# A fused attention and feed-forward kernel on one core: weight conversion listed as seven single operations, the first two parts of w_in by column halves, and the list in another order

## The chip, the cores and the metric

The kernel runs on one core of a Trainium2 chip. The time is the device time of one execution in microseconds (us), as the median of several runs. The core has a matrix engine (TensorE, PE in the profile, with PEld for its weight loads), a vector engine (VectorE, DVE), a scalar engine (ScalarE, ACT), a general one (GpSimd, POOL) and an engine that issues transfers (SyncE, SP). Each works through its own queue in order and waits on semaphores for the others. Operands stand in on-chip memory (SBUF), matmul results in banks of PSUM; transfers from and to DRAM are DMAs.

## The reference

```python
# attention: q, k, v, alpha of shape (4, 8, 768, 48), float32
for t in range(S):
    state = alpha[:, :, t, :, None] * state + np.einsum('bhd,bhe->bhde', k[:, :, t], v[:, :, t])
    y[:, :, t] = np.einsum('bhd,bhde->bhe', q[:, :, t], state)
# bridge: (B,H,S,D) -> (B*S, H*D), 3072 tokens of 384
x = attn_out.transpose(0, 2, 1, 3).reshape(B * S, H * D)
# feed-forward: w_in (384, 2048) and w_out (2048, 384), float64
h = np.maximum(x @ w_in, 0.0)
return (h * h @ w_out).astype(np.float32)
```

The state decays by alpha in each row and step, so a chunk of 128 steps is computed at once with cumulative sums of log(alpha).

## The kernel before, in words

**Blocks and groups.** The attention is cut into 24 blocks n: chunk n // 4 of 128 time steps of batch n % 4. Four blocks are a group g of 512 tokens, the unit of the feed-forward part; there are six groups. All 24 blocks of a head's state go in sequence for their batch, so block n needs the state that block n - 4 left.

**The list.** The program is one list of words, `ORDER`, such as `load:5:q` or `ha:0`. A word names a step, a Python function that issues a few instructions, and its numbers. The list is run once from front to back, with the scheduler in manual mode, so the list is the order of each engine's queue; there is no planner and no cost in the kernel. What the list can't say are the waits: they follow from the data, from the rotation of buffers, and from one more rule. The loads of blocks 4 to 7 and all loads of w_in parts are `behind_newest`: they wait until the TensorE instruction that was listed last before them has run.

**Steps of a block.** `load:n:a`, `:q`, `:k`, `:v` are the loads on SyncE. `ln` (ScalarE) takes the log of alpha, `cs` (TensorE) sums it along time, `eb` and `ei` (ScalarE, L540) give exp of plus and minus the sum, `mq` and `mk` (VectorE, L548) scale q and k by them, `dl`, `de`, `bl`, `br` carry the last row. `qT`, `kT` and `turned_one` transpose on TensorE, `qc`, `kc` and `half_copied` (ScalarE) copy the result out of PSUM. `sc` and `kv` (TensorE) are scores and state sums, `one_masked` (VectorE) masks scores, `us`, `sa`, `sb` (VectorE, L705) update the state. `y_states`, `y_inner`, `yb` (TensorE) give y for a pair of blocks, and twelve `moved:n:p:i` (ScalarE, L779) copy that y, transposed, into x, the input of the feed-forward part, for the pair n and n + 1.

**Weights.** w_in and w_out come as eight parts each (0 to 7 are w_in, 8 to 15 w_out). `load_weights:i` brings a part of 768 KB into one of four raw buffers. As the engines have no float64, the conversion works on the two 32-bit words of each number, for all 768 numbers of a partition at once: `first` is two VectorE operations on the high word (the exponent, L422, and the mantissa bits, L426), `middle` two ScalarE operations (the exponent moved up, L435, and the low word scaled, L438), `second` three VectorE operations (the sign, L444, the two mantissa words joined, L448, the product, L451).

**Feed-forward.** Group 0 has its first layer in plain fp32 matmuls: `ha:j` for the first 256 tokens (blocks 0 and 1), `hb:j` for the others, `hf:j` for all 512; `ra`, `rb`, `rf` and `qa`, `qb`, `qf` are relu and square on ScalarE. j is one of 16 slices of the hidden layer; j // 2 is the part of w_in that it needs. Some later j of group 0, and all of the other groups, are split into faster fp32r matmuls: `cast_w`, `rest_w`, `diff_w` make three pieces of a weight part (`wb`, `wl`, `wd`), `split_x`, `rest_x`, `diff_x` three of x, and `in_x` and `in_y` multiply them. `in_scaled`, `in_added`, `in_post`, `in_square` finish h, `split_h`, `rest_h`, `diff_h` split it (`ha`, `hl`, `hd` in the profile), and `out_x`, `out_y` are the second layer, with `out_plain` as its fp32 form. `kept_l`, `kept_d` and `fetch` move pieces of the weights to DRAM and back. `warm` is a dummy matmul of the start. All matmuls are recorded at line L350, a wrapper, so they are told apart by the names of their tiles.

In this kernel the first 13 `warm` steps stand ahead of the first `ha`, and conversion of part 0 stands after `y_inner:0`. The buffers: 4 raw, 26 for weight parts (`wt`), 22 for pieces of h (`two`), 2 for `upper`, 8 banks of PSUM.

Of the kernel before, what the change touches and what calls it, by code (L numbers as in the profile page):

```python
# [36 lines left out]
half_copied:q:5:0 half_copied:q:5:1 sc:5 kv:5 load:8:a load:7:k load:7:q split_x:0:0 rest_x:0:0 split_x:0:1  # L37
first:5 rest_x:0:1 cast_w:i:4 split_x:0:2 rest_x:0:2 one_masked:5:0 half_copied:q:6:0 half_copied:k:6:0
load:6:v hb:2 ei:7 diff_x:0:0 rf:6 first:6 one_masked:5:1 us:5 rb:5 qb:5 qa:4 diff_x:0:1 diff_x:0:2 qa:1 hf:7
y_states:4 mk:7 y_inner:4 rb:2 ln:8 sa:5 half_copied:k:6:1 half_copied:q:6:1 sc:6 load:9:a log_high:8 eb:7  # L40
mq:7 turned_one:7 log_rest:8 kv:6 bl:7 rf:7 middle:6 half_copied:k:7:0 second:6 half_copied:q:7:0 hb:4
load:8:k ln:9 log_high:9 half_copied:k:7:1 one_masked:6:1 load:8:q log_rest:9 cs:8 eb:8 ei:8 load:9:k
rest_w:i:4 load:9:q load:7:v hb:1 cs:9 bl:8 mk:8 rb:4 rb:1 half_copied:q:7:1 mq:8 one_masked:6:0 kept_l:i:4
ei:9 load:10:a us:6 eb:9 mk:9 cast_w:i:6 bl:9 hb:3 rb:3 load:11:a turned_one:8 sc:7 mq:9 rest_w:i:6
half_copied:q:8:0 half_copied:q:8:1 half_copied:k:8:0 half_copied:k:8:1 load_weights:7 yb:4 kv:7 turned_one:9
middle:5 diff_w:i:4 kept_d:i:4 in_x:8 half_copied:q:9:0 sa:6 load:10:q kept_l:i:6 diff_w:i:6 kept_d:i:6
half_copied:k:9:0 ln:10 in_x:12 ln:11 second:5 in_x:13 log_high:10 log_rest:10 load_weights:8 one_masked:7:1
one_masked:7:0 in_scaled:8 in_y:8 us:7 log_high:11 half_copied:q:9:1 in_scaled:12 in_scaled:13 cast_w:i:5
first:7 br:4 log_rest:11 sa:7 in_y:12 in_y:13 in_x:9 rest_w:i:5 in_post:12 half_copied:k:9:1 middle:7 cs:11
load:8:v eb:11 in_post:8 second:7 cs:10 ei:10 eb:10 in_scaled:9 kept_l:i:5 diff_w:i:5 kept_d:i:5 in_x:10  # L50
in_scaled:10 in_x:11 in_y:9 cast_w:i:7 rest_w:i:7 qb:0 moved:4:0:0 moved:4:0:1 kept_l:i:7 in_y:10 in_post:10
diff_w:i:7 kept_d:i:7 in_x:14 in_square:12 in_x:15 first:8 in_scaled:11 in_y:11 sb:4 load_weights:9
in_scaled:14 in_y:14 middle:8 moved:4:0:2 in_added:13 in_added:9 moved:4:1:0 moved:4:1:1 in_added:11 second:8
ei:11 moved:4:1:2 in_scaled:15 y_states:6 y_inner:6 moved:4:2:0 moved:4:2:1 sc:8 moved:4:2:2 moved:4:3:0 br:5
load:10:k yb:6 kv:8 qb:1 qb:2 moved:4:3:1 one_masked:8:0 bl:11 moved:4:3:2 one_masked:8:1 us:8 qb:3 first:9
middle:9 moved:6:0:0 in_y:15 in_added:15 moved:6:0:1 moved:6:0:2 second:9 load_weights:10 first:10 moved:6:1:0
# [210 lines left out]
def kernel(  # L267
# [144 lines left out]
    def convert_first(i):  # L412
        if moe_w_in.dtype == FP32:
            return
# [686 lines left out]
```

## Time and profile before

| | us |
|---|---|
| median of 3 runs | 519.35 |
| lowest and highest run | 519.31, 520.91 |
| profiled execution, whole time | 521.08 |
| profiled execution, span from first to last instruction | 519.30 |
| TensorE busy, of the span | 508.6 (98%) |
| VectorE busy | 362.6 (70%) |
| ScalarE busy | 314.4 (61%) |
| chain that ended last: TensorE's share of the span | 88% |
| chain that ended last: VectorE, ScalarE, DMA | 4%, 3%, 2% |
| TensorE clock granted, mean over the span | 0.997 |

The busy time of an engine says how full it was on average, and not which one was late at a given place. For that, the stretches of the span (busy time of each engine in each), the groups of equal instructions with their mean duration, and the instructions of an engine in order of time with what they waited for are read together. In a row of the groups stand the line, the engine, the operation, output and inputs with their shapes and the count; then the busy time in all and the mean of one in ns; then the idle time of the engine just before them and what ended it. In a row of the timeline stand the start and the duration in us, and in brackets the idle time before and what ended it.

### The profile page before, as it was taken

What the parts mean: (1) busy time and instruction counts of PE and PEld (TensorE: products, weight loads), DVE (VectorE), ACT (ScalarE), POOL (GpSimd) and SP (SyncE); (2) the same over time, 40 slices, a digit from 0 to 9 for tenths busy, and PEclk for the clock granted to TensorE, in tenths of its full rate; (3) what the DMA queues carried; (4) which work ended last, traced back from release to release, by engine and by line L of the source; (5) the groups of instructions that cost most, each with busy time, mean ns of one, the idle gap of its engine ahead of it and who ended that gap; (6) DMA issues with size and microseconds to landing.
All of it is one profiled execution on the core that took longest, in us unless ns stands there. A gap on an engine that the chain in (4) does not pass through costs nothing.

```text
span 519.3 us, 13138 instructions
## 1 busy us (share of the span) xinstructions
PE 508.6 (98%) x5404; PEld 432.0 (83%) x5404; DVE 362.6 (70%) x629; ACT 314.4 (61%) x681; POOL 5.4 (1%) x29
## 2 busy tenths in 40 slices
PE   8989999999999999999999999999999999999997
PEld 6676788567778879987899988899987899988997
DVE  3678999998988898635998147597344598126961
ACT  4789999977486673058766247765253775324620
POOL 4000000000000000000000000000000000000000
PEclk9989999999999999999999999999999999999999
DMA  9969898977756668698876479756883744579301
GB/s 161 218 174 249 176 266 269 275 236 217 220 170 196 193 219 255 215 308 199 239 185 184 146 230 287 216 153 174 221 259 124 231 136 143 182 273 404 123 0 61
DMA packets 140762, 106.27 MB, mean 205 GB/s; under 512 B 109968, under 2 KB 113056, under 8 KB 140704
## 3 DMA queue, kind: packets, MB, share of 16 engines
q1 hardware_dynamic: 140704, 105.45, 70.1%
q8 instruction: 42, 0.69, 0.6%
q14 instruction: 16, 0.13, 0.1%
HBM read 88.10 MB, written 17.33 MB: 203 GB/s over the span
## 4 chain that ended last, share of the span: by engine, by line
PE 88%; DVE 4%; ACT 3%; DMA 2%; issue 1%; POOL 0%; DVEq 0%; ACTq 0%; POOLq 0%
PE o L350 40%; PE h L350 36%; PE sckv L350 4%; PE y L350 4%; PE cs L350 2%; PE T L350 2%; DMA a_in<-in_alpha_dram 1%; PE warm L350 1%; DMA q_in<-in_q_dram 1%; ACT x L779 1%; DVE hid L802 1%; DVE power L444 1%; DVE w_out L451 0%; DVE w_in L451 0%; DVE w_out L448 0%
## 5 line engine op out<-in xcount | busy, mean ns | idle before, releaser
L350 PE MATMUL h<-xa,wb 128*128 128x512 f32 x264 | 76.4, 397 | 0.8 <-ACT ks L754 0.6
L350 PE MATMUL h<-xl,wl 128*128 128x512 f32 x264 | 74.5, 390 | 0.0
L350 PE MATMUL h<-xd,wd 128*128 128x512 f32 x264 | 69.6, 397 | 0.0
L779 ACT COPY x<-y 32x256 f32<-32x256 f32 (+3 forms) x144 | 50.9, 366 | 16.9 <-PE y L350 14.6
L350 PEld LDWEIGHTS h<-xa,wb 128*128 128x128 f32 x264 | 48.8, 188 | 12.3 <-ACT ks L754 1.0
L350 PEld LDWEIGHTS h<-xl,wl 128*128 128x128 f32 x264 | 49.6, 188 | 11.0 <-DVE xl L848 0.2
L350 PEld LDWEIGHTS h<-xd,wd 128*128 128x128 f32 x264 | 48.7, 188 | 11.0 <-ACT h L900 0.5
L802 DVE TENSOR_TENSOR hid<-h,hid 128x512 f32<-128x512 f32 x44 | 29.7, 687 | 40.2 <-PE h L350 40.1
L350 PE MATMUL o<-wb,ha 128*128 128x384 f32 x168 | 56.9, 339 | 0.1
L350 PE MATMUL o<-wd,hd 128*128 128x384 f32 x320 | 56.9, 334 | 0.0
L350 PE MATMUL o<-wl,hl 128*128 128x384 f32 x168 | 56.2, 335 | 0.0
L350 PEld LDWEIGHTS o<-wd,hd 128*128 128x128 f32 x320 | 55.7, 188 | 0.3
L350 PE MATMUL o<-wb,hx 128*128 128x384 f32 x152 | 51.2, 337 | 0.0
L350 PE MATMUL o<-wl,hx 128*128 128x384 f32 x152 | 50.8, 334 | 0.0
L898 ACT ACTIVATE hid<-h 128x512 f32<-128x512 f32 x44 | 26.3, 598 | 38.8 <-PE h L350 38.7
L923 ACT ACTIVATE hid<-h 128x512 f32<-128x512 f32 x44 | 25.8, 598 | 36.4 <-PE h L350 36.1
L802 DVE TENSOR_TENSOR osb<-o,osb 128x384 f32<-128x384 f32 x24 | 12.9, 555 | 44.7 <-PE o L350 30.9
L350 PE MATMUL o<-w_out,hid 128*128 128x384 f32 x128 | 44.0, 491 | 0.0
L845 ACT ACTIVATE ha<-hid 128x512 fp32r<-128x512 f32 x42 | 26.1, 632 | 22.4 <-DVE hid L918 12.0
L900 ACT ACTIVATE h<-h 128x512 f32<-128x512 f32 x44 | 25.6, 591 | 22.8 <-PE h L350 22.6
L350 PEld LDWEIGHTS o<-w_out,hid 128*128 128x128 f32 x128 | 23.7, 189 | 15.9 <-DVE w_out L451 1.0
L848 DVE SCALAR_TENSOR_TENSOR hl<-ha,hid 128x512 fp32r<-128x512 f32 x42 | 28.3, 686 | 12.1 <-ACT ha L845 11.9
(113 smaller groups left out, 893.2 us busy)
## 6 DMA issues: line engine op xcount, KB each, us to landing
wd<-do SPq DMA_DIRECT2D x38, 384.0 KB
wd<-di SPq DMA_DIRECT2D x36, 384.0 KB
wl<-li SPq DMA_DIRECT2D x36, 384.0 KB
wl<-lo SPq DMA_DIRECT2D x34, 384.0 KB
raw<-in_moe_w_in_dram SPq DMA_DIRECT2D x8, 768.0 KB
raw<-in_moe_w_out_dram SPq DMA_DIRECT2D x8, 768.0 KB
v_in<-in_v_dram SPq DMA_DIRECT2D x24, 192.0 KB
out_dram<-osb SPq DMA_DIRECT2D x24, 192.0 KB
```

The costliest lines, as they stand in the source:

```text
L350: newest[:] = [f(*args, **kwargs)]
L444: nc.vector.scalar_tensor_tensor(out=power, in0=hi, scalar=0x80000000, in1=power, op0=ALU.bitwise_and, op1=ALU.bitwise_or,)
L779: copy(out=xT[g][kk].rearrange("a (t c) -> a t c", c=C)[to : to + m, t : t + 2], in_=blk[n]["y"][e][r : r + m, :, p // 2],)
L802: nc.vector.tensor_tensor(out=o, in0=x, in1=z, op=op)
L845: nc.scalar.activation(out=a, in_=x, func=AF.Copy, scale=NEAR * E)
L848: nc.vector.scalar_tensor_tensor(out=l, in0=a.bitcast(FP32), scalar=-1.0 / E, in1=x, op0=ALU.mult, op1=ALU.add)
L898: nc.scalar.activation(out=hid[j], in_=x, func=AF.Copy, scale=E)
L900: nc.scalar.activation(out=x, in_=x, func=AF.Copy, scale=1.0 + E)
L923: nc.scalar.activation(out=h, in_=acc.pop(("h", j)), func=AF.Relu)
```

## The change

`load_weights` becomes `part_loaded:i:h`, and the three conversion steps become seven, one for each instruction: `exponent`, `mantissa` (VectorE), `moved_up`, `lower` (ScalarE), `signed`, `joined`, `valued` (VectorE). Each takes h: 0 and 1 are the left and the right half of the part's columns, 2 is the whole part. In the new list parts 0 and 1 are loaded and converted as halves (two DMAs and fourteen instructions for each, on 384 elements per partition), parts 2 to 15 as wholes. What each instruction computes is the same.

Copies, relus and squares now go through helpers (`copied_to`, `positive_to`, `squared_to`) which give them to the other engine if a word ends with `~`. No word of the new list does, so each stays on the engine it was on; the entries of `AT` that could do the same for a few copies, and left them all on ScalarE, are gone.

The list is written anew: 2428 words for 2348. The words that are not about conversion or weight loads are the same as before, each as many times; their order is another from the first word to the last. All 16 `warm` steps now stand ahead of the first `ha` (13 before). Old and new beginning, up to the copies of the second pair, and the functions:

```diff
 ORDER = """
-load:0:a warm:0 warm:0 warm:0 load:1:a warm:0 ln:0 load:0:q ln:1 warm:0 cs:0 eb:0 load:0:k mq:0 load:1:k cs:1
-ei:0 dl:0 load:0:v qT:0 de:0 warm:0 load:3:a load:1:q mk:0 kT:0 qc:0 kc:0 sc:0 kv:0 load:1:v load:2:a
-one_masked:0:1 load_weights:0 load:2:q load:4:a ei:1 mk:1 one_masked:0:0 eb:1 mq:1 ln:3 us:0 cs:3 ei:3 sa:0
-sb:0 dl:1 kT:1 load:2:k load:5:a kc:1 qT:1 qc:1 sc:1 load:3:q load:3:k kv:1 one_masked:1:0 warm:0 ln:2 cs:2
-ei:2 warm:0 eb:2 one_masked:1:1 load:2:v warm:0 warm:0 eb:3 us:1 y_states:0 y_inner:0 warm:0 mq:2 qT:2 ln:4
-first:0 middle:0 dl:3 load:4:q mk:2 de:1 second:0 cs:4 eb:4 load_weights:1 yb:0 load:4:k load:3:v ei:4 qc:2
-dl:2 kT:2 mk:3 mq:3 ln:5 warm:0 cs:5 de:2 kc:2 sc:2 kv:2 one_masked:2:1 moved:0:0:0 warm:0 moved:0:0:1
-moved:0:0:2 mq:4 load_weights:2 moved:0:1:0 kT:3 moved:0:1:1 moved:0:1:2 moved:0:2:0 moved:0:2:1 de:3
-moved:0:2:2 moved:0:3:0 qT:3 moved:0:3:1 moved:0:3:2 one_masked:2:0 us:2 sa:2 sb:2 load:7:a ha:1 ha:0 bl:4
-warm:0 first:1 mk:4 turned_one:4 kc:3 qc:3 middle:1 load:6:a second:1 ra:0 load_weights:3 ra:1 sc:3 qa:0
-half_copied:q:4:0 half_copied:q:4:1 eb:5 bl:5 kv:3 one_masked:3:0 load:5:k half_copied:k:4:0 half_copied:k:4:1
-warm:0 first:2 warm:0 middle:2 ln:6 ha:3 one_masked:3:1 ha:2 ra:2 ei:5 us:3 cs:6 load:5:q load:4:v y_states:2
-y_inner:2 sc:4 ln:7 load_weights:4 second:2 qa:2 eb:6 load:6:k sa:3 load:6:q ei:6 sa:1 first:3 ra:3 ha:4
-load_weights:5 sb:1 qa:3 mk:5 middle:3 ra:4 sb:3 yb:2 moved:2:0:0 mq:5 moved:2:0:1 moved:2:0:2 moved:2:1:0
-moved:2:1:1 cs:7 moved:2:1:2 moved:2:2:0 moved:2:2:1 moved:2:2:2 turned_one:5 kv:4 second:3 ha:5
-one_masked:4:0 one_masked:4:1 moved:2:3:0 moved:2:3:1 moved:2:3:2 first:4 us:4 half_copied:k:5:0 middle:4 mk:6
-hb:0 bl:6 load:5:v second:4 load_weights:6 hf:6 rb:0 ra:5 qa:5 hb:5 sa:4 mq:6 turned_one:6 half_copied:k:5:1
...
+warm:0 warm:0 load:0:v load:0:a ln:0 cs:0 ei:0 eb:0 load:0:q load:1:a warm:0 load:0:k warm:0 ln:1 load:3:a
+mk:0 dl:0 de:0 load:1:k mq:0 ln:3 load:1:q load:2:a warm:0 load:1:v load:4:a kT:0 warm:0 kc:0 qT:0 qc:0 cs:1
+load:2:k ei:1 eb:1 load:2:q part_loaded:0:0 part_loaded:0:1 cs:3 eb:3 sc:0 kv:0 mq:1 qT:1 dl:1 load:5:a
+load:3:k ln:2 cs:2 one_masked:0:1 one_masked:0:0 us:0 ei:2 sa:0 sb:0 warm:0 mk:1 kT:1 qc:1 kc:1 warm:0 mk:2
+load:3:q load:2:v warm:0 part_loaded:1:0 sc:1 kv:1 one_masked:1:0 one_masked:1:1 us:1 part_loaded:1:1 ei:3
+eb:2 mq:2 ln:4 cs:4 mantissa:0:0 dl:2 load:6:a lower:0:0 joined:0:0 exponent:0:0 eb:4 de:1 ln:5 dl:3 de:3 qT:2
+mk:3 warm:0 warm:0 exponent:0:1 moved_up:0:1 signed:0:1 kT:2 load:3:v kc:2 mantissa:0:1 load:4:q mq:3
+part_loaded:2:2 qc:2 ei:4 bl:4 mantissa:1:0 y_states:0 de:2 y_inner:0 yb:0 moved:0:0:0 exponent:1:0 lower:0:1
+joined:0:1 warm:0 kT:3 moved:0:0:1 moved:0:0:2 kc:3 moved:0:1:0 valued:0:1 moved_up:1:0 load:4:k warm:0 cs:5
+part_loaded:3:2 signed:1:0 moved_up:0:0 signed:0:0 moved:0:1:1 valued:0:0 qT:3 qc:3 exponent:1:1 moved:0:1:2
+sc:2 kv:2 one_masked:2:0 lower:1:0 mantissa:1:1 one_masked:2:1 load:7:a load:5:k warm:0 joined:1:0
+moved_up:1:1 signed:1:1 lower:1:1 joined:1:1 moved:0:2:0 load:5:q valued:1:0 warm:0 warm:0 load:6:k
+moved:0:2:1 moved:0:2:2 moved:0:3:0 moved:0:3:1 moved:0:3:2 ln:6 us:2 sc:3 kv:3 one_masked:3:0 one_masked:3:1
+ha:0 sa:2 us:3 sa:3 valued:1:1 exponent:2:2 load:4:v sb:2 mantissa:2:2 lower:2:2 ei:5 eb:5 ha:1 ha:2 ha:3
+part_loaded:4:2 part_loaded:5:2 cs:6 mk:4 moved_up:2:2 ra:1 qa:1 joined:2:2 ra:2 mq:4 turned_one:4 y_states:2
+mantissa:3:2 lower:3:2 y_inner:2 yb:2 half_copied:k:4:0 eb:6 half_copied:q:4:0 ln:7 cs:7 exponent:3:2
+signed:2:2 valued:2:2 ra:0 ha:5 half_copied:k:4:1 mk:5 moved:2:0:0 sa:1 half_copied:q:4:1 load:6:q
+part_loaded:6:2 mq:5 sb:1 moved_up:3:2 signed:3:2 bl:5 moved:2:0:1 sb:3 moved:2:0:2 moved:2:1:0 joined:3:2
+ei:6 moved:2:1:1 sc:4 kv:4 ha:4 bl:6 ra:3 moved:2:1:2 moved:2:2:0 ra:5 load:5:v load:8:a moved:2:2:1
+one_masked:4:1 moved:2:2:2 moved:2:3:0 moved:2:3:1 qa:5 moved:2:3:2 one_masked:4:0 valued:3:2 us:4
+turned_one:5 exponent:4:2 half_copied:k:5:0 load:7:q sa:4 ra:4 hb:5 mantissa:4:2 half_copied:q:5:0 mk:6
+lower:4:2 joined:4:2 load:7:k moved_up:4:2 signed:4:2 qa:0 split_x:0:0 rest_x:0:0 valued:4:2 load:6:v
+mantissa:5:2 split_x:0:1 hb:1 lower:5:2 qa:3 hb:0 rb:0 mq:6 br:4 qa:2 hf:6 rb:1 load:9:a hb:2 rest_x:0:1
...
 """
...
-    def load_weights(i):
+    def part_loaded(i, h):
         dt = moe_w_in.dtype
         shape = (KM, DF // NW) if i < NW else (NJ // NW, DM)
         if dt == FP32:
             raw = target(i)
         else:
-            raw = raw_pool.tile([128, *shape], dt, tag="raw", name="raw")
-        raws[i] = raw
+            if i not in raws:
+                raws[i] = raw_pool.tile([128, *shape], dt, tag="raw", name="raw")
+            raw = raws[i]
         if i < NW:
-            src = moe_w_in[:, i * DF // NW : (i + 1) * DF // NW]
-            behind_newest(nc.sync.dma_start(out=raw, in_=src.rearrange("(k r) f -> r k f", r=128)))
+            cols = columns(i, h)
+            src = moe_w_in[:, i * DF // NW + cols.start : i * DF // NW + cols.stop]
+            behind_newest(nc.sync.dma_start(out=raw[:, :, cols], in_=src.rearrange("(k r) f -> r k f", r=128)))
         else:
             i -= NW
             src = moe_w_out[i * DF // NW : (i + 1) * DF // NW, :]
             nc.sync.dma_start(out=raw, in_=src.rearrange("(j r) m -> r j m", r=128))
...
+    over = [False]
+    def copied_to(out, x, scale=1.0, vector=False):
+        if vector == over[0]:
+            if scale == 1.0:
+                nc.scalar.copy(out=out, in_=x)
+            else:
+                nc.scalar.activation(out=out, in_=x, func=AF.Copy, scale=scale)
+        elif scale == 1.0:
+            nc.vector.tensor_copy(out=out, in_=x)
+        else:
+            nc.vector.tensor_scalar(out=out, in0=x, scalar1=scale, scalar2=None, op0=ALU.mult)
...
+    def columns(i, h):
+        n = DF // NW if i < NW else DM
+        return slice(0, n) if h == 2 else slice(h * n // 2, (h + 1) * n // 2)
+    def wide(x, i, h):
+        shape = (KM, DF // NW) if i < NW else (NJ // NW, DM)
+        if x in "lo hi":
+            t = raws[i].bitcast(U32).rearrange("a k (f h) -> a k f h", h=2)[:, :, :, x == "hi"]
+        elif x == "w":
+            t = target(i)
+        else:
+            if (x, i) not in half:
+                half[x, i] = (
+                    wt("power", U32, shape) if x == "power"
+                    else cv_pool.tile([128, *shape], U32, tag="upper", name="upper")
+                )
+            t = half[x, i]
+        return t if h == 2 and x in ("w", "power", "upper") else t[:, :, columns(i, h)]
+    def exponent(i, h):
         nc.vector.tensor_scalar(
+            out=wide("power", i, h), in0=wide("hi", i, h), scalar1=20, scalar2=0x7FF,
             op0=ALU.logical_shift_right, op1=ALU.bitwise_and,
         )
+    def mantissa(i, h):
         nc.vector.tensor_scalar(
+            out=wide("upper", i, h), in0=wide("hi", i, h), scalar1=0xFFFFF, scalar2=None, op0=ALU.bitwise_and
+        )
+    def moved_up(i, h):
+        power = wide("power", i, h)
+        nc.scalar.activation(out=power, in_=power, func=AF.Relu, scale=2.0**23, bias=rebias)
+    def lower(i, h):
+        w, lo = wide("w", i, h), wide("lo", i, h)
+        if over[0]:
+            nc.vector.tensor_scalar(out=w, in0=lo, scalar1=2.0**-52, scalar2=1.0, op0=ALU.mult, op1=ALU.add)
+        else:
+            nc.scalar.activation(out=w, in_=lo, func=AF.Copy, scale=2.0**-52, bias=1.0)
+    def signed(i, h):
+        power = wide("power", i, h)
         nc.vector.scalar_tensor_tensor(
+            out=power, in0=wide("hi", i, h), scalar=0x80000000, in1=power,
             op0=ALU.bitwise_and, op1=ALU.bitwise_or,
         )
+    def joined(i, h):
+        w = wide("w", i, h)
         nc.vector.scalar_tensor_tensor(
+            out=w, in0=wide("upper", i, h), scalar=2.0**-20, in1=w, op0=ALU.mult, op1=ALU.add
+        )
+    def valued(i, h):
+        w = wide("w", i, h)
+        nc.vector.tensor_tensor(out=w, in0=w, in1=wide("power", i, h).bitcast(FP32), op=ALU.mult)
...
-    steps["first"], steps["middle"], steps["second"] = convert_first, convert_middle, convert_second
...
-        f, *given = word.split(":")
+        f, *given = word.rstrip("~").split(":")
+        over[0] = word.endswith("~")
```

More of the change, by code (lines that the diff above doesn't have):

```diff
@@ L45 @@
[L45 to L54, printed above, removed]
@@ new lines @@
+one_masked:8:1 moved:4:2:0 moved:4:2:1 in_scaled:15 moved:4:2:2 moved:4:3:0 qb:1 cast_w:i:2 fetch:l:i:5
+in_y:14 in_y:15 out_plain:0:0:6 one_masked:8:0 us:8 fetch:d:i:7 mq:10 load:11:k in_post:14 out_plain:0:2:6
+part_loaded:11:2 exponent:9:2 moved_up:9:2 mantissa:9:2 lower:9:2 bl:11 in_added:15 out_plain:0:3:6
+moved:4:3:1 signed:9:2 out_plain:0:1:6 joined:9:2 valued:9:2 qb:4 moved:6:0:0 load:11:v moved:6:0:1
+moved:6:0:2 part_loaded:12:2 qb:5 fetch:d:i:6 moved:6:1:0 moved:6:1:1 qb:3 out_plain:1:0:6 moved:6:1:2
@@ new lines @@
+fetch:l:i:6 moved:6:2:0 moved:6:2:1 mk:10 out_plain:1:3:6 load:13:a exponent:10:2 load:12:a moved:6:2:2
+out_plain:1:1:6 sa:8 rest_w:i:1 kept_l:i:1 moved_up:10:2 moved:4:3:2 moved:6:3:0 br:7 br:8 mantissa:10:2
+lower:10:2 out_plain:1:2:6 moved:6:3:1 moved:6:3:2 qf:7 mk:11 mq:11 signed:10:2 turned_one:11
+half_copied:q:11:0 half_copied:q:11:1 joined:10:2 valued:10:2 mantissa:11:2 lower:11:2 exponent:11:2
+turned_one:10 half_copied:k:10:0 out_plain:2:1:6 in_post:9 rest_w:i:2 kept_l:i:2 half_copied:k:10:1
@@ L753, in half_copied @@
             blk[n][f"{x}s"] = work(f"{x}s", 2 if x == "k" else 4)
-        nc.scalar.copy(out=blk[n][f"{x}s"][:, :, HALF[h]], in_=blk[n]["T"][h][:, "kq".index(x)])
-    SHARED = {(n, int(p)) for n, ps in enumerate(AT["shared"].split(",")) for p in ps}
+        copied_to(blk[n][f"{x}s"][:, :, HALF[h]], blk[n]["T"][h][:, "kq".index(x)])
     def cells(p):
```

507 lines of the change are left out of this document (244 added, 263 removed).

## The prediction

> **What bounds the kernel now.** I read first the engines' busy time, then the same by stretches of the span, because an average over stages with different limits hides where time is lost, and last the chain that ended last. The first line below is the page's; the others are the stretches (span, then each engine's busy time with its count, clock, DMA share, GB/s) and their sum.
>
> ```profile
> PE 508.6 (98%) x5404; PEld 432.0 (83%) x5404; DVE 362.6 (70%) x629; ACT 314.4 (61%) x681; POOL 5.4 (1%) x29
> ...
> 0.00:10.00 10.00, 7.91 (x56) 5.86 (x60) 2.92 (x5) 5.04 (x11) 5.36 (x29) 1.00 1.04 157
> 10.00:20.00 10.00, 9.29 (x235) 7.05 (x226) 5.88 (x15) 5.72 (x13) 0.00 (x0) 1.00 1.11 215
> 20.00:30.00 10.00, 8.01 (x152) 5.72 (x152) 7.14 (x14) 8.70 (x26) 0.00 (x0) 0.95 0.91 200
> 30.00:40.00 10.00, 10.00 (x122) 7.99 (x124) 7.35 (x12) 7.42 (x17) 0.00 (x0) 0.88 0.64 185
> 40.00:50.00 10.00, 9.22 (x198) 7.17 (x193) 7.93 (x17) 9.29 (x24) 0.00 (x0) 1.00 1.00 223
> 50.00:60.00 10.00, 9.60 (x126) 5.94 (x128) 9.96 (x20) 9.94 (x27) 0.00 (x0) 1.00 0.92 219
> 60.00:70.00 10.00, 10.00 (x304) 8.93 (x296) 9.96 (x19) 8.74 (x23) 0.00 (x0) 1.00 0.85 178
> 70.00:80.00 10.00, 9.96 (x57) 8.03 (x58) 9.97 (x17) 9.63 (x21) 0.00 (x0) 1.00 1.03 317
> 90.00:100.00 10.00, 10.00 (x67) 5.60 (x59) 8.84 (x18) 9.72 (x22) 0.00 (x0) 1.00 1.10 258
> 100.00:120.00 20.00, 20.00 (x157) 13.16 (x156) 18.71 (x29) 16.51 (x36) 0.00 (x0) 1.00 0.74 229
> 160.00:200.00 40.00, 39.42 (x421) 33.12 (x421) 37.51 (x65) 25.06 (x54) 0.00 (x0) 1.00 0.73 224
> 500.00:519.30 19.30, 15.90 (x92) 15.58 (x90) 4.15 (x8) 2.27 (x5) 0.00 (x0) 1.00 0.11 41
> sum 519.30, PE 508.57 PEld 431.96 DVE 362.55 ACT 314.40 POOL 5.36; mean PE 22.11 PEld 18.78 DVE 15.76 ACT 13.67 POOL 0.23
> ```
>
> TensorE (PE) is busy 508.57 of 519.30 us. Its first 60 us hold 54.03 (7.91 + 9.29 + 8.01 + 10.00 + 9.22 + 9.60), so 5.97 idle; the last stretch lacks 3.40, which is the last copy and the store; the 440 us between hold 438.64, so 1.36 idle. The change neither adds nor removes a matmul, so only three things can move: the start, stalls hidden inside "busy" groups, and 1.36 us. What follows TensorE in the start is seen in the other columns: from 50 us on VectorE (DVE) is busy 8.84 to 9.97 of each 10 us and ScalarE (ACT) 8.74 to 9.94, while before that VectorE idles 18.78 of 50 us. VectorE stays near full up to 200 us (18.71 of 20, 37.51 of 40). So the helpers' late start is never made up before the second group of tokens: a microsecond saved on VectorE or ScalarE before 50 us is worth up to a microsecond at the end, and one lost costs the same.
>
> How much TensorE could win at most comes from long unbroken stretches of the chain:
>
> ```profile
> 458.01 21.80 PE h L350 x96
> ...
> 490.22 25.70 PE o L350 x148
> ```
>
> A split matmul of 512 columns costs 21.80 / 96 = 0.227 us, one of 384 costs 25.70 / 148 = 0.174 us. With these, and stretches found in the same way for the small ones, the whole list sums to some 495 us, 6.9 of them the 16 `warm` steps (an estimate). Against 516 us at the last matmul about 20 us are lost, some 16 of them before 90 us. Where, is seen in the instructions in order of time:
>
> ```profile
> 21.74 0.96 DVE L451 TENSOR_TENSOR w_in<-w_in,power 128x768 f32<-128x768 f32 x1
> 28.75 0.56 DVE L422 TENSOR_SCALAR power<-raw 128x768 uint32<-128x768 uint32 x1 [0.66 <-DMA raw<-in_moe_w_in_dram]
> 29.04 4.40 PE L350 MATMUL h<-x,w_in 128*128 128x256 f32 x12
> 36.49 2.75 PE L350 MATMUL h<-x,w_in 128*128 128x256 f32 x12
> 39.92 0.37 SPq L376 DMA_DIRECT2D q_in<-in_q_dram  x1
> 44.19 4.37 ACT L779 COPY x<-y 32x256 f32<-32x256 f32 x12
> 44.97 0.56 DVE L548 TENSOR_TENSOR q_in<-q_in,b 128x384 f32<-128x384 f32 x1 [2.01 <-DMA q_in<-in_q_dram]
> 45.58 0.46 PE L350 MATMUL T<-ident,q_in 64*128 64x64 f32 x8 [0.78 <-DVE q_in L548]
> 47.30 0.96 DVE L451 TENSOR_TENSOR w_in<-w_in,power 128x768 f32<-128x768 f32 x1
> ```
>
> The same 12 instructions of the first layer take 4.40 us at 29.04 and 2.75 at 36.49; the stretch between shows a clock of 0.95 and 0.88, so 1.65 us went to a slow clock and late inputs. The first `ha` waits for the twelve copies `moved:0`, not for weights (the last operation on part 0 ends at 21.74 + 0.96 = 22.70). The load of q for block 5 is issued only at 39.92, because it is ordered behind a matmul listed late; it keeps VectorE waiting 2.01 us at 44.97 and TensorE 0.78 at 45.58. The second half of the tokens, `hb`, waits for the copies `moved:2`, which end at 44.19 + 4.37 = 48.56. Part 3 of w_in is converted at 47.30 + 0.96 = 48.26.
>
> **The change, part by part: halves.** Two parts get twice the instructions. The grouped rows (mean ns) and two neighbouring pairs:
>
> ```profile
> L444 DVE SCALAR_TENSOR_TENSOR power<-raw,power 128x768 uint32<-128x768 uint32 x16 | 15.3, 956 | 4.7 <-ACT power L435 4.5
> L422 DVE TENSOR_SCALAR power<-raw 128x768 uint32<-128x768 uint32 x16 | 8.9, 555 | 0.7 <-DMA raw<-in_moe_w_in_dram 0.7
> L435 ACT ACTIVATE power<-power,rebias 128x768 uint32<-128x768 uint32 x16 | 15.1, 945 | 3.7 <-DVE power L422 3.7
> L548 DVE TENSOR_TENSOR k_in<-k_in,inv 128x384 f32<-128x384 f32 x23 | 12.7, 553 | 0.4 <-DMA k_in<-in_k_dram 0.3
> L540 ACT ACTIVATE b<-cs 128x384 f32<-128x384 f32 x24 | 11.8, 495 | 5.9 <-PE cs L350 5.8
> L705 DVE TENSOR_TENSOR s<-s,last 128x192 f32<-128x192 f32 x20 | 7.1, 353 | 0.2
> ...
> 66.45 0.55 DVE L548 TENSOR_TENSOR k_in<-k_in,inv 128x384 f32<-128x384 f32 x1
> 66.92 0.55 DVE L548 TENSOR_TENSOR q_in<-q_in,b 128x384 f32<-128x384 f32 x1
> ...
> 71.79 0.95 DVE L444 SCALAR_TENSOR_TENSOR power<-raw,power 128x768 uint32<-128x768 uint32 x1
> 72.66 0.96 DVE L448 SCALAR_TENSOR_TENSOR w_in<-upper,w_in 128x768 f32<-128x768 uint32 x1
> ```
>
> Queued back to back, a two-input operation on 384 elements takes 66.92 - 66.45 = 0.47 us and on 768 takes 72.66 - 71.79 = 0.87. Two halves cost 0.94, 0.07 more; three such operations on two parts: 0.4 us. No row shows the one-input form (555 ns) on 384 elements: two halves cost between the whole's price (nothing more) and twice it (0.47 back to back, so 0.47 more). I take a half at 0.30, near the 353 ns of the 192-element row, which makes 0.13 more, times two operations and two parts: 0.5 us. VectorE therefore gets 0.9 us more (0.4 to 2.3). On ScalarE two of 495 stand against one of 945 ns: 4 x 0.05 = 0.2 us. The two extra DMA issues lie on SyncE, which is ahead of the data there.
>
> [...]
>
> **The start in the new order.** Counted in the order of the lists (a block load is 128 x 384 fp32, 196.6 KB, a part 384 x 256 float64, 786.4 KB), part 0 is not early: its last byte is number 3,342 KB in the new load order against 2,752; part 1, 4,914 against 5,111; part 2, 6,290 in both; part 3, 7,273 against 7,469. The three first stretches carry 157, 215 and 200 GB/s, so part 0 lands at about 20 us and part 1, by its row, near 28 (28.75 now). What moves is the gating: q of block 5 stands behind TensorE work of 21.7 us instead of 30.0, so the 2.01 and 0.78 us waits should go. Three waits come in: ScalarE's `ln:5` now stands ahead of `qc:2`, `ei:4` and the first `moved_up` and waits for its load to about 21 us; `mk:3` on VectorE waits for k to about 22, and `mantissa:1:0` for half a part to about 26, with `joined:0:1`, `valued` and the state updates queued behind. Walking the new list with the quoted durations, `moved:0` ends at 32.8 instead of 29.2, so `ha:0` begins some 3 us later than now. But then `ha:0` to `ha:3` run in one piece, with both parts converted and all `warm` steps spent; `yb:2` ends near 40.7 and the 12 `moved:2` copies at 46.8 instead of 48.56, with the same ScalarE work before them (38.0 against 38.1 us of summed durations). That is 1.8 us. VectorE has part 3 converted at 46 to 47.6, 0.7 to 2.3 us earlier, though more work lies ahead (32.8 against 30.3): its idle time falls by about 3 us. I take 1.8, ScalarE's figure, since `hb` needs both.
>
> **From 50 to 200 us.** The new order puts more VectorE work ahead of the same TensorE progress: 104.8 against 102.9 us of summed durations ahead of the first split matmul of token group 1, 157.5 against 154.6 near 151 us of TensorE work. Durations overlap (all sum to 397 us, and the engine is busy 362.55), so these are 1.7 and 2.6 us. The halves' 0.9 is in them. Set against 3 us less idle time, VectorE ends 0.4 to 1.3 us ahead. ScalarE needs 1.5 to 2 us more before the group 1 matmuls near 64 us, against 1.8 won. So of the early gain something between 0 and 1.8 us lives to 200 us; I take 1.0. Splitting each conversion in seven lets other work stand between its operations in both engines; in the old list `second` is three operations in a row (L444, L448 and L451, about 0.96 us each by the rows above) that a k or q scaling must wait out, and TensorE waits for such (0.78 above). The stretches from 60 us hold 1.36 us of named idle time and about 3 us hidden in groups; I take 1.0 off for that, bounds 1.5 us more and 3 off. After 200 us VectorE has slack and both lists do the same work at the same TensorE progress within 4 us, so nothing is taken.
>
> Sum: 1.0 + 1.0 = 2.0 us off. The profiled execution took 521.08 us, its span 519.30 with 1.78 around it; it lies 1.73 above the median of 519.35. So 519.1 for a profiled run like it, and 517.3 for the median.
>
> **Rivals.** *VectorE becomes the bound up to 190 us.* If the three new waits cost what the freed loads save, its idle time stays at 18.8 of the first 50 us, and the 2.6 us of work put ahead is paid in full by `out_x` and `out_y` of group 0: 519.35 + 2.6 = 522.0, up to 526 if `mantissa:1:0` waits 3 us longer than worked out or the one-input halves take 2.3 us. It decides from the point where VectorE's idle time before 50 us exceeds 18. For it: VectorE is at 37.51 of 40 between 160 and 200 us. Against: the 2.01 us wait has a cause that the list removes. 0.35.
>
> *The early gain is absorbed:* TensorE enters group 1 at the time it does now because ScalarE, 9.72 busy between 90 and 100 us, is the limit, and its work did not shrink: 519.3, within 1.5. [...] 0.17.
>
> *The order closes nearly all gaps before 200 us:* both slow groups and the hidden stalls, 7 us: 512.4. For it: 20 us are lost in all. Against: both helpers are full. 0.10.
>
> **Numbers.** About 0.3%, 1.6 us, is what a measurement can tell from no change. The forecast holds 0.38, its own range 515.5 to 518.5; a little of it and most of the absorbed case lie within 0.3%. That gives faster 0.46, same 0.17, slower 0.37. The range from 512 to 526 leaves out half of the large gain and the tail of the slow rival.
>
> **What would show it.** Right: `ha:0` near 32 to 33 us with `ha:1` to `ha:3` behind it without a gap; no DMA wait of 2 us on q; `moved:2` done before 47.5; VectorE idle under 17 us in the first 50; TensorE's busy sum near 507. Wrong: `moved:2` later than 48.6, VectorE idle above 18 us by 50, or TensorE waiting for `hl`, `hx` or `wl` between 100 and 200 us by more than 2 us in all, which is the first rival.

## The result, and the profile after

The changed kernel takes 523.20 us (median of 6 runs, 521.42 to 524.11); the kernel before took 519.33 in the same runs (6 runs). The ratio is 1.0067, with a 95% interval of 1.0044 to 1.0091: slower by some 3.5 us by that ratio (3.9 between the medians), where 517.3 was forecast. The profiled execution of the changed kernel took 524.11 us, the slowest of its six, and its span was 522.30.

The page's busy times and its shares of the chain that ended last, and the same stretches as before (span, then busy time and count of TensorE, its weight loads, VectorE, ScalarE and GpSimd, clock, DMA share, GB/s):

```profile
PE 511.1 (98%) x5404; PEld 432.0 (83%) x5404; DVE 362.0 (69%) x639; ACT 317.1 (61%) x685; POOL 5.3 (1%) x29
...
PE 80%; ACT 9%; DVE 6%; DMA 3%; issue 1%; SPq 0%; DVEq 0%
```

```profile
0.00:10.00 10.00, 6.73 (x28) 4.33 (x29) 2.86 (x5) 3.54 (x8) 5.33 (x29) 1.00 1.05 156
10.00:20.00 10.00, 9.81 (x112) 6.84 (x110) 3.27 (x8) 4.86 (x11) 0.00 (x0) 1.00 1.20 215
20.00:30.00 10.00, 9.87 (x273) 7.99 (x274) 6.65 (x16) 8.04 (x23) 0.00 (x0) 1.00 0.84 193
30.00:40.00 10.00, 8.25 (x121) 6.72 (x114) 9.59 (x24) 9.74 (x23) 0.00 (x0) 1.00 1.07 258
40.00:50.00 10.00, 9.35 (x212) 6.96 (x210) 9.25 (x19) 8.64 (x23) 0.00 (x0) 1.00 0.78 218
50.00:60.00 10.00, 9.91 (x111) 7.10 (x111) 8.07 (x14) 9.93 (x25) 0.00 (x0) 1.00 0.78 171
100.00:200.00 100.00, 98.98 (x993) 74.96 (x991) 91.70 (x149) 70.07 (x141) 0.00 (x0) 1.00 0.67 204
```

TensorE is idle 6.08 us in the first 60 (5.97 before), and its busy time is 2.5 us more for the same matmuls: the loss sits inside "busy" groups. VectorE is busy 31.62 of the first 50 us, so 18.38 idle (18.78 before); the prediction had drawn its line at 17 for right and 18 for wrong. ScalarE is the one that falls behind: 34.81 busy by 50 us against 36.17, and 9% of the chain that ended last instead of 3%.

The instructions of the start in order of time:

```profile
1.09 2.08 PE L361 MATMUL warm<-s 128*128 128x256 f32 x4 [1.09 <-POOL s L319]
5.34 1.62 PE L361 MATMUL cs<-a_in,causal 128*128 128x384 f32 x2 [2.17 <-ACT a_in L555]
...
10.34 1.06 PE L361 MATMUL kT<-ident,k_in 128*128 128x128 f32 x4
...
35.09 5.45 PE L361 MATMUL h<-x,w_in 128*128 128x256 f32 x24 [0.90 <-ACT x L420]
33.64 2.18 ACT L420 COPY x<-y 32x256 f32<-32x256 f32 x6
...
50.75 0.36 ACT L420 COPY x<-y 16x256 f32<-16x256 f32 x1
43.97 0.55 DVE L603 TENSOR_TENSOR q_in<-q_in,b 128x384 f32<-128x384 f32 x1
...
48.18 0.95 DVE L506 TENSOR_TENSOR w_in<-w_in,power 128x768 f32<-128x768 f32 x1
```

Four dummy matmuls stand ahead of the first `cs` and not ten, and TensorE then idles 2.17 us for alpha of block 0, because the new list loads v first. The four transposes at 10.34 take 1.06 us (four such take 0.60 in a run below). The first `ha` waits for a copy of `moved:0`, and these end at 33.64 + 2.18 = 35.82. `ha:0` to `ha:3` run without a gap, as forecast, and `mq:5` at 43.97 waits for no load. But the copies `moved:2` end at 50.75 + 0.36 = 51.11 (46.8 forecast, 48.56 before), and part 3 is converted at 49.13 (48.26 before).

### The profile page after: what moved, and what is told of

The parts are those of the page before. It is cut to its first block, busy times and chain, and to the rows that moved or that the text cites. A ratio compares the mean times of both kernels' runs of the same rounds, so it can differ in the third digit from the quotient of the medians.

```text
span 522.3 us, 13135 instructions
## 1 busy us (share of the span) xinstructions
PE 511.1 (98%) x5404; PEld 432.0 (83%) x5404; DVE 362.0 (69%) x639; ACT 317.1 (61%) x685; POOL 5.3 (1%) x29
## 4 chain that ended last, share of the span: by engine, by line
PE 80%; ACT 9%; DVE 6%; DMA 3%; issue 1%; SPq 0%; DVEq 0%
PE o L361 38%; PE h L361 31%; ACT x L420 3%; PE sckv L361 3%; PE y L361 3%; PE cs L361 2%; PE T L361 1%; DMA raw<-in_moe_w_out_dram 1%; ACT power L482 1%; PE warm L361 1%; DMA wd<-di 1%; DMA a_in<-in_alpha_dram 1%; DVE am L711 1%; DVE w_in L500 1%; DVE power L470 1%
## 5 line engine op out<-in xcount | busy, mean ns | idle before, releaser
L420 ACT COPY x<-y 32x256 f32<-32x256 f32 (+1 forms) x144 | 50.8, 366 | 18.3 <-PE y L361 15.4
```

The source lines that it names most:

```text
L420: nc.scalar.copy(out=out, in_=x)
```

## The experiments

**Which half of the list, and what of it are the halves?** The first four kernels took the change apart: halves without the new order, the new order without halves, and lists joined from the two at some 40 us. All grafts are in the code of the changed kernel. Each ratio here and below is against the kernel before, run beside it; the runs come from several chips, so ratios and not microseconds are compared between them, and a "give or take" is what the two 95% intervals make together.

```diff
 e1: the old list; first:0 -> exponent:0:0 exponent:0:1 mantissa:0:0 mantissa:0:1, and so on for parts 0 and 1
 e2: the new list; of part_loaded:0:0 ... part_loaded:0:1 only part_loaded:0:2, at the second place, and so on
 e3: old list up to ha:2 (as e1), then all other words as the new list has them
 e4: new list up to ha:3, then all other words as the old list has them (as e1)
```

> The old order, with parts 0 and 1 loaded and converted as halves, each pair of halves where the whole stood; parts 2 to 15 as wholes. Theory A (the loss comes from the new order of the start, before the first four ha): halves cost VectorE up to 0.9 us in a stretch where it idles, 519.3 to 520.2. Rival B (the halves themselves bring the loss): 521.5 to 523.

> The new order, with parts 0 and 1 as wholes, each step at the place of the second of its halves. Theory A: within 1 us of the changed kernel, 522 to 524, since the copies that the first ha waits for come late with or without halves. Rival B: back to 519.5 to 520.5.

> The old order up to its ha:2 (187 words, some 40 us; parts 0 and 1 as halves), then all other words in the order of the new list. Theory A: two of the 3.5 us go, 520.5 to 521.5, and TensorE stands about 1 us behind the old kernel after 100 us. Rival C (what is lost is VectorE's greater load between 50 and 190 us): 522 to 523.5.

> The new order up to its ha:3 (181 words, some 40 us), then all other words in the order of the old list. Theory A: 521 to 522, two thirds of the loss. Rival C: 519.3 to 520.

Measured: e1 521.20 us, ratio 1.0032 (1.0015 to 1.0048); e2 525.32, 1.0110 (1.0085 to 1.0135); e3 522.89, 1.0073 (1.0049 to 1.0097); e4 523.23, 1.0087 (1.0065 to 1.0110). By the medians the halves cost in the old order, and in the new they save some 2 us: neither theory A nor rival B had that. But 5 of e1's 12 executions and 3 of e2's 6 have a granted clock of 0.997 or less (0.997 is that of the profiled execution of the kernel before, in which, as comes up again below, 3.41 us run at half speed), against 2 of 17 of the kernel before beside them. The other 7 of e1 have a median of 519.65, so neither difference is the price of the halves alone. e3 and e4 are each as slow as the whole change, so the parts do not add up. Two more grafts went the same way.

```diff
 e7: old list up to ha:2, parts 0 and 1 whole, then the new list's order
 e8: old list up to turned_one:11 (some 101 us), parts whole, then the new list's order
```

> The old order up to its ha:2 with parts 0 and 1 as wholes, as in the kernel before (187 words, some 40 us), all other words in the order of the new list. If halves cost 1.7 us in the old start, as the first runs had it, and the rest of the new list 1.7: 521. If the new rest is all of the loss: 523. If it costs nothing by itself: 519.5.

> The old order up to its turned_one:11 (some 101 us), parts 0 and 1 as wholes, then all other words in the order of the new list. If the loss of the new rest lies between 40 and 105 us (conversion of parts 8 to 10 of the weights later, four stalls of 0.5 us before them): 519.3 to 520. If it lies behind 105 us: as e7.

Measured: e7 522.39, 1.0066 (1.0049 to 1.0083); e8 523.28, 1.0092 (1.0069 to 1.0115). By its expectation e8 would put the loss behind 105 us. Its waits (who waited for whom in a window: us in total, times, longest) say otherwise, and so do those of e4:

```profile
PE o L358 <- DVE w_out L503: 2.9, 1, 2.9
```

```profile
PE h L361 <- DVE w_in L506: 2.6, 1, 2.6
```

Right behind the cut TensorE waits 2.9 us (e8) and 2.6 us (e4) for a conversion that the one list would have had done and the other not yet asks for. The grafts measure their own seam, and 10 of the 24 executions of e3, e4, e7 and e8 have a clock of 0.997 or less. They are inconclusive on where the loss is; the repairs below, each a few words inside the new list, say more.

**TensorE's slow start.** Two more `warm` at the very front; and, alone, the first load of v behind the first load of k.

```diff
 e5
+warm:0 warm:0
 warm:0 warm:0 load:0:v load:0:a ln:0 cs:0 ...
 e6
-warm:0 warm:0 load:0:v load:0:a ... load:0:k warm:0
+warm:0 warm:0 load:0:a ... load:0:k load:0:v warm:0
```

> The new order with two more warm steps (four dummy matmuls) at its very front, nothing else changed. Theory D (the new start leaves TensorE idle for 2.17 us between its first four dummy matmuls and the first cs, so that it stays slow until 9 to 14 us, and what follows comes later): the first matmuls run at full speed by 6 to 7 us, 521 to 522. Rival E (the late first load and the order after it decide, not TensorE's speed): within 0.7 us of the changed kernel, 522.5 to 524.

> The new order with the first load of v moved behind the first load of k, so that alpha of block 0 is the first load as in the old order. Theory D: the gap before the first cs falls from 2.17 to about 1 us, the first ln starts near 3.5 us; 521.5 to 523. Rival E: the whole chain of block 0 comes 1.2 us earlier, 521.5 to 522.5. If the start does not reach the end: 523.

Measured: e5 521.32 (520.88 to 522.28), 1.0054 (1.0038 to 1.0070); e6 523.56, 1.0081 (1.0060 to 1.0103). TensorE, VectorE and ScalarE of e5 in order of time:

```profile
1.10 3.53 PE L361 MATMUL warm<-s 128*128 128x256 f32 x8 [1.10 <-POOL s L319]
5.20 0.88 PE L361 MATMUL cs<-a_in,causal 128*128 128x384 f32 x2 [0.58 <-ACT a_in L555]
...
9.83 0.60 PE L361 MATMUL qT<-ident,q_in 128*128 128x128 f32 x4
...
33.51 5.45 PE L361 MATMUL h<-x,w_in 128*128 128x256 f32 x24 [0.89 <-ACT x L420]
22.46 0.56 DVE L603 TENSOR_TENSOR qk_lent<-qk_lent,inv 128x384 f32<-128x384 f32 x1 [1.58 <-DMA qk_lent<-in_k_dram]
22.94 0.42 DVE L470 TENSOR_SCALAR power<-raw 128x384 uint32<-128x384 uint32 x1
23.39 0.61 ACT L482 ACTIVATE power<-power,rebias 128x384 uint32<-128x384 uint32 x1 [1.83 <-DVE power L470]
...
49.16 0.36 ACT L420 COPY x<-y 16x256 f32<-16x256 f32 x1
```

The first `cs` takes 0.88 instead of 1.62 us, and four transposes 0.60 instead of 1.06. The first `ha` comes 1.6 us earlier and `moved:2` at 49.52 instead of 51.11, as theory D has it. But not every execution of the new start is so slow. The clock record, the trace's list of stretches at full and at half speed, has full speed from 14.13 us in the changed kernel, and from 8.67 in e4, whose list begins with the same 181 words. There the first `ha` comes as early as in e5, without the two `warm`:

```profile
33.37 5.45 PE L361 MATMUL h<-x,w_in 128*128 128x256 f32 x24 [0.91 <-ACT x L420]
```

So the 1.6 us are the price of a clock that came late in one execution. With eight dummy matmuls at the front it was early in all six profiles (4.2 to 7.3 us). By all runs e5 is 0.13% below the changed kernel, give or take 0.28: alone, the two `warm` bring nothing that can be told from noise. In e6 the first load is the old one, with four dummy matmuls ahead of `cs`. Its profiled execution has the first `ha` at 32.58, and then runs 6.83 us at half speed from 31.12 on; its other five, at a clock of 1.00, have a median of 523.50. Why nothing is won there stays open.

**A wait ahead of part 0.** The rows above show the next one: ScalarE waits 1.83 us for `exponent:0:1` (L470), which stands behind `mk:3` (L603), which waits 1.58 us for k of block 3. The prediction had named `mk:3` and `mantissa:1:0` as new waits. In the profile of the changed kernel itself `mk:3` comes later and waits for nothing, because what stands ahead of it was late already (VectorE's wait of 2.26 us for TensorE's scores ends at 21.31 us there; the same wait, of 2.25, ends at 18.60 in e4):

```profile
24.05 0.54 DVE L603 TENSOR_TENSOR qk_lent<-qk_lent,inv 128x384 f32<-128x384 f32 x1
```

So the late clock and the wait for k cover each other, and repairing one alone shows the other. A second place lies at 100 to 106 us, where part 10 of the weights is converted among the copies of x:

```profile
104.36 0.96 DVE L500 SCALAR_TENSOR_TENSOR w_out<-upper,w_out 128x768 f32<-128x768 uint32 x1 [0.74 <-ACT w_out L489]
106.37 4.14 PE L361 MATMUL o<-w_out,hid 128*128 128x384 f32 x12 [0.49 <-DVE w_out L506]
```

```profile
101.13 0.96 DVE L505 TENSOR_TENSOR w_out<-w_out,power 128x768 f32<-128x768 f32 x1
102.62 4.14 PE L360 MATMUL o<-w_out,hid 128*128 128x384 f32 x12
```

The first fence is of the changed kernel: VectorE waits 0.74 us for ScalarE's `lower:10`, and TensorE 0.49 us for the part. The second is of e10, where neither waits.

```diff
 e9: e5, and
-de:3 qT:2 mk:3 warm:0 warm:0 exponent:0:1 moved_up:0:1 ... mantissa:1:0 ... joined:0:1
+de:3 qT:2 exponent:0:1 mk:3 warm:0 warm:0 moved_up:0:1 ... joined:0:1 mantissa:1:0
 e10: e9, and
+exponent:10:2 mantissa:10:2 moved_up:10:2 lower:10:2
 out_plain:1:0:6 moved:6:1:2 ... (taken out at their eight copies further on)
 e15: the new list with only that change of e10
```

> The new order with the two more warm steps, and two words moved: exponent:0:1 ahead of mk:3, which waits 1.58 us for the load of k of block 3, and mantissa:1:0, which waits 1.04 us for its half part, behind joined:0:1. If ScalarE's wait of 1.83 us for exponent:0:1 is what makes the copies for the first ha late: 520 to 520.8 (0.5 to 1.3 less than with the two warm steps alone). If ScalarE would have waited for the copies' y anyway: 521.3.

> As the run before it, and the first four operations of part 10 of the weights moved ahead of the first out_plain:1, so that they stand before eight copies of x and not between them. If TensorE's wait for part 10 near 106 us (0.49 us, and 0.5 us hidden in the matmuls behind it) reaches the end: 0.5 to 1 us less than the run before. If another word of those twelve copies is then late (the transposes behind them wait for them): no less.

> The new order with part 10 moved and nothing else. If each place has its own price that reaches the end: 522 to 522.6. If TensorE waits for part 10 only because it is earlier there after the other repairs: 523.2.

Measured: e9 520.87, 1.0034 (1.0023 to 1.0045); e10 520.03, 1.0020 (1.0005 to 1.0035); e15 522.77, 1.0066 (1.0042 to 1.0090). e9 is 0.20% below e5 (give or take 0.19). Its first `ha` is at 31.90, 1.6 us ahead of e5's. e10's median is 0.8 us below e9's, run beside it, but 0.14% give or take 0.19 is not clear of noise; in the two profiles e10 has its first `ha` 0.6 us later and still a span 0.7 us shorter. Part 10 alone (e15) brings nothing that can be seen in the total. Its profiled execution has no wait for part 10, but another one ahead of it:

```profile
86.94 0.96 PE L360 MATMUL h<-xl,wl 128*128 128x512 f32 x3 [0.81 <-DVE wl L863]
```

The changed kernel waits 0.19 us there. In e15 VectorE had waited 0.94 us for a load of w_out just before, and 0.31 in the changed kernel. So six runs of e15 cannot price part 10.

**The rest.** From e10 one thing was taken or added at a time.

```diff
 e12: e10 without the two more warm
 e13: e10 with load:0:v behind load:0:k
 e14: e10 with parts 0 and 1 whole (as in e2)
 e17: e13 with load:2:k ahead of load:4:a
```

> The new order with the two words and the four operations of part 10 moved as in the two runs before it, but without the two more warm steps. If TensorE's slow start costs the end 1 to 2 us by itself: 521 to 522. If it only mattered while the other two places were slow: 520 to 520.5.

> The new order with all three repairs (two more warm steps, the two words, part 10), and the first load of v behind the first load of k. If what is left of the loss, some 1 us, comes from the first load, with which ScalarE and all behind it start 1.2 us later: 519 to 519.6. If the start has slack once TensorE is fast: 520.

> The new order with all three repairs, parts 0 and 1 as wholes, each step where its second half stood. If halves only add instructions (0.9 us of VectorE): 519.3 to 520. If they start part 0 and part 1 earlier, as the 2.1 us between the new order with and without halves said: 521 to 522.5.

> The new order with the three repairs and the old first load, and load:2:k ahead of load:4:a, as VectorE still waits for k of the first blocks. If the start of the helpers still sets the end: 518.5 to 519.3, less than the kernel before. If the start is no longer late: 519.6, as without it.

Measured: e12 521.94, 1.0051 (1.0033 to 1.0070); e13 519.63, 1.0011 (0.9999 to 1.0023); e14 521.67, 1.0056 (1.0036 to 1.0077); e17 520.08, 1.0009 (0.9996 to 1.0022). So without the two `warm` the repaired list is 0.31% slower (give or take 0.24). The profiled execution of e12 does not show the start as the reason. Its clock was up at 8.60 us, its first `ha` comes 0.2 us before e10's, and what it loses it loses later, in waits for pieces of the weights (this one, and 0.5 us for `wd`; e10 waits 0.2 in all for such pieces):

```profile
32.27 5.45 PE L360 MATMUL h<-x,w_in 128*128 128x256 f32 x24 [1.17 <-ACT x L419]
312.79 0.96 PE L360 MATMUL h<-xl,wl 128*128 128x512 f32 x3 [0.98 <-DMA wl<-li]
```

Whether the clock was late in other executions of e12, no run shows, so the 0.31% has no shown cause. With the old first load as well, the new list is no longer distinguishable from the old one (e13); moving one more of the first loads gives nothing (e17). The halves are worth 0.36% in this order (e14 against e10, give or take 0.25); e14's profile has ScalarE busy 36.41 of the first 50 us and e10's 37.88, as if work on a first half filled time that a whole part leaves empty. That this is the reason was not tried.

**The yardstick.** Two runs in the old order, and its own instructions once more in the code of the changed kernel (e0).

```diff
 e11: the old list, the warm ahead of moved:0:0:1 with four more matmuls into its bank
 e16: the old list
+load:5:q
 ha:1 ha:0 ... (taken out ahead of load:4:v)
```

> The old order in the code of the changed kernel: the seven single operations stand where the three steps stood, all parts as wholes, so each engine gets the instructions of the kernel before in the same order. 519.2, within 0.5 us of the kernel before, by every theory.

> The old order, with two more dummy matmul pairs into the bank of the warm step ahead of moved:0:0:1, where TensorE idles 1.54 us before it falls to half speed for 3.41 us in some runs. If that idle time causes the slow stretch: no run below a clock of 0.998, and a median of 518.5 to 519. If not: 519.2 and the same share of runs at 0.997.

> The old order with one word moved, load:5:q ahead of ha:1, so that it waits for TensorE's instruction ahead of ha:1 and not for the one ahead of its old place. If the waits of 2.01 us (VectorE) and 0.78 us (TensorE) near 45 us were worth what the prediction took for them: 0.5 to 1 us under the kernel before. If the load then collides with those of parts 2 and 3 of the weights: 519.2 or slower.

Measured: e0 518.99, 1.0006 (0.9990 to 1.0022), so the code without the list costs nothing; e11 520.20, 1.0019 (1.0006 to 1.0032); e16 519.68, 1.0012 (1.0000 to 1.0025). From e0's profile, `ha:1` and `ha:0`, VectorE's `mq:5`, and the copies `moved:2`, with the stretch of the kernel before that differs:

```profile
29.37 2.76 PE L359 MATMUL h<-x,w_in 128*128 128x256 f32 x12
42.34 0.55 DVE L601 TENSOR_TENSOR q_in<-q_in,b 128x384 f32<-128x384 f32 x1
43.02 4.36 ACT L418 COPY x<-y 32x256 f32<-32x256 f32 x12
```

```profile
28.00:32.00 4.00, 4.00 (x15) 3.16 (x15) 2.39 (x5) 3.90 (x8) 0.00 (x0) 0.62 0.85 243
```

The profiled execution from which the prediction was made ran at a clock of 0.62 between 28 and 32 us; its clock record has 3.41 us at half speed there. In e0, with the same instructions at full speed, `ha:1` and `ha:0` take 2.76 us and not 4.40, q of block 5 is there in time with no word moved, and `moved:2` ends at 47.38, not 48.56. The load of q waits for TensorE, and TensorE was slow. e16 frees a wait that e0's profile does not have either, and gains nothing. e11 filled the idle time ahead of that stretch: its 12 runs all have a granted clock of 0.999 or more, where the kernel before, run beside it, has 3 of 34 at 0.997 or less (14 of 102 beside all runs). With so few, 12 runs without one do not prove that the idle time brings the stretch. The stretch is too rare to matter for the median of the kernel before, and e11 as a whole is 0.19% slower; that its added matmuls cost this is likely, but was not tried.

All repairs together, by the profiled execution of each (one execution; ratio from all runs):

| kernel | ratio | full speed from | ScalarE busy by 50 us | first `ha` at | `moved:2` ends |
|---|---|---|---|---|---|
| old order, e0 | 1.0006 | 6.22 | 37.75 | 29.37 | 47.38 |
| new order | 1.0067 | 14.13 | 34.81 | 35.09 | 51.11 |
| e5, two more `warm` | 1.0054 | 4.23 | 36.65 | 33.51 | 49.52 |
| e9, and two words | 1.0034 | 5.95 | 38.31 | 31.90 | 47.92 |
| e10, and part 10 | 1.0020 | 6.06 | 37.88 | 32.50 | 48.51 |
| e13, and the old first load | 1.0011 | 7.23 | 38.52 | 31.69 | 47.71 |
| e12, e10 without the two `warm` | 1.0051 | 8.60 | 38.11 | 32.27 | 48.30 |

The stretch up to 50 us of the new order (and the one behind it), of e0 and of e13:

```profile
0.00:50.00 50.00, 44.02 (x725) 32.83 (x725) 31.62 (x70) 34.81 (x84) 5.33 (x29) 1.00 0.99 208
50.00:105.00 55.00, 54.68 (x753) 40.08 (x753) 50.72 (x86) 52.87 (x120) 0.00 (x0) 1.00 0.89 246
```

```profile
0.00:50.00 50.00, 44.60 (x735) 33.34 (x736) 32.97 (x63) 37.75 (x89) 5.36 (x29) 1.00 0.98 204
```

```profile
0.00:50.00 50.00, 46.25 (x742) 35.27 (x743) 33.12 (x73) 38.52 (x91) 5.36 (x29) 1.00 1.02 226
```

ScalarE's work by 50 us (fourth figure) is 2.94 us less in the new order than in the old one, and 0.77 more after the repairs. After that ScalarE is full: 52.87 of the 55 us up to 105 in the changed kernel.

## Why the prediction was wrong

**The start: the step that failed.** "`moved:0` ends at 32.8" was 35.82, and the copies `moved:2`, forecast at 46.8, ended at 51.11. The traces take the 3.0 us of `moved:0` apart. In e4, which has the same start with the clock up earlier, it ends at 34.09 (31.91 + 2.18), so some 1.7 us are the late clock. In e9, where the clock is early and ScalarE does not wait behind `mk:3`, it ends at 32.63, what the walk had:

```profile
30.45 2.18 ACT L420 COPY x<-y 32x256 f32<-32x256 f32 x6
```

Of `moved:2`, 47.92 in e9, 1.1 us stay unexplained. This is the slowest execution of six; how late the start is in the median one is not known. The walk priced every instruction with its duration at full speed. It did not see that the new list gives TensorE only four dummy matmuls before its first real one and then leaves it idle for a load that was moved to second place. The words were in the list; the prediction counted the 16 `warm` ahead of the first `ha` and not where they stood. The clock records have full speed from 14.13 us in the changed kernel, and from 8.60 to 8.73 in e12, e4 and e2, whose lists begin with the same words; from 4.2 to 6.7 in the lists that begin with ten dummy matmuls. So the same beginning reached full speed at 8.60 us in one execution and at 14.13 in another, 5.5 us apart; a slow stretch inside a run took 3.41 us in the kernel before and 6.83 in e6. What sets the moment, no run shows.

**The new waits were named, but not what ScalarE pays for them.** The prediction listed `mk:3` waiting to about 22 us (22.46 in e5), and the walk had this wait and that of `mantissa:1:0` on VectorE only. Behind `mk:3` stood `exponent:0:1`, and behind that ScalarE's `moved_up`: 1.83 us of ScalarE in e5. Taking both words out of the way was worth 0.20% (1.0054 to 1.0034, give or take 0.19).

**The gain was read off a disturbed execution.** The 1.8 us for `moved:2` was 48.56 less 46.8. Against 47.38, the old order at full speed, 0.6 would have been left. The waits of 2.01 and 0.78 us did go, as forecast, but e0 has them neither, so nothing was won by it. The hint stood in the rows: a clock of 0.88 between 30 and 40 us, and a profiled execution 1.73 us over the median. The prediction put 1.65 us of the first `ha` down to a slow clock and late inputs, and subtracted the 1.73 at the end, but did not take them out of the 48.56.

**Splitting the conversions: no gain seen.** The forecast took 1.0 us off because other work can stand between the seven operations. In part 10 three copies of x stood between its first four operations and three more ahead of them, and TensorE waited 0.49 us for the part. Closing that up took 0.8 us off the median once the start was repaired, as said not clear of noise; no run shows a gain from the splitting.

**The halves.** VectorE's 0.9 us came from rows for two operands (0.07 each) and a guess of 0.30 us for one operand on 384 elements. The row was:

```profile
L470 DVE TENSOR_SCALAR power<-raw 128x384 uint32<-128x384 uint32 x4 | 1.7, 418 | 0.0
L500 DVE SCALAR_TENSOR_TENSOR w_in<-upper,w_in 128x384 f32<-128x384 uint32 x4 | 2.2, 553 | 0.8 <-ACT w_in L489 0.7
```

0.418 us, inside the bounds; queued, these operations start 0.33 us apart (26.89 and 27.22 us in the changed kernel), so two halves take 0.66 where a whole takes 0.47 (40.92 and 41.39 in the kernel before). In the old order the halves cost 0.32%, 1.7 us, by all runs, but the executions of e1 with a clock above 0.997 have a median only 0.4 us above that of such executions of the kernel before (519.65 and 519.24). In the new order the halves save. Their price could not be read without the order around them.

**The rival that had the number had another mechanism.** The first rival forecast 522.0 to 526 with VectorE as the bound up to 190 us, decided by more than 18 us of idle time before 50. The time and the 18.38 us came out so. But e13 keeps the order from 50 to 190 us but for four operations of part 10, with all the VectorE work put ahead there, and is within 0.11% of the old kernel. In the changed kernel TensorE waits 1.02 us in all between 100 and 200 us (1.02 is 100 less its busy 98.98), less than the 2 us that the prediction set for that rival. That its number came out was luck. Instead, in the profiled executions, the late start carried the result (the first `ha` at 35.09, and 31.90 in e9), with the wait for k in it and part 10 behind it, and ScalarE handed it on: busy 52.87 of 55 us, it could not catch up. e9's span ends 3.4 us before the changed kernel's (518.9 and 522.3), as much as its first `ha` was ahead (3.2). That these repairs and the old first load together bring the tie is measured (1.0067 to 1.0011); what each is worth alone is not, as most steps between lie within the noise.

Right were the run of four `ha`, the wait for q that vanished, and, as far as a tie can show it, that the list behind 200 us wins or loses nothing: e13 keeps all of it and ties with the old one. No version beats the kernel before.

## What to carry to other kernels

Look first whether the profiled execution stands for the median: compare the durations of equal instructions, and take a stretch at a lower clock out of the rows before a gain is measured against it. The same holds for the profile after: that of the changed kernel was the slowest of six, and part of what the first repair seemed to win was only that. In a new list read the first ten instructions of each engine as closely as the place that the change is about: in the clock records given here full speed begins at 4.2 to 7.3 us where eight or ten dummy matmuls stand ahead of the first real one, and at 8.60 to 14.19 where four do, and ScalarE, busy 52.87 of the 55 us behind the start, did not make up what was lost there. And to locate a loss, repair a few words inside the new order; joining two orders tuned as wholes brought waits at the seam of 2.9 and 2.6 us here, where 3.5 were sought.

## What the runs showed of the hardware that was not expected

The whole stretches in the clock records have lengths with a common measure: 3.41 us at half speed (the kernel before), 6.83 at half speed (e6), 23.89 and 488.11 at full speed (the kernel before) and 508.59 at full speed (the changed kernel) are 1, 2, 7, 143 and 149 times 3.4133. The granted clock of the stretches does not show all of it: in the changed kernel it reads 1.00 from 0 to 20 us, while four transposes take 1.06 us instead of 0.60. e15, whose start is the same, has full speed from 14.19 us, and both profiled executions are the slow ones of their six runs (524.11 of 521.42 to 524.11, 524.61 of 520.81 to 524.61); the profiled executions of e2, e4 and e12, with full speed from 8.6 to 8.7, are not. That would make the moment at which full speed begins a large part of the spread between runs of one kernel, but e12 lost 1.5 us in waits for `wl` and `wd` as well, and runs without a profile have no such record, so this stays open.
